# RWKV-6 attention followed by a squared-ReLU MLP on one core: another way to column sums, and a new written-out order

## The chip, the cores and the metric

The kernel runs on one core of a Trainium2 chip. A core has five engines that run side by side, each with its own in-order queue of instructions: TensorE (PE, matrix products), VectorE (DVE), ScalarE (ACT), GpSimd (POOL) and SyncE (SP), which here only issues transfers. The metric is the time on the device in microseconds (us), a median over runs. A profile is taken of one further execution. Its span runs from the first to the last instruction of the program.

## What is computed

The inputs r, k, v, w have the shape (4 batches, 8 heads, 768 steps, 48). For each batch and head a 48 x 48 state is carried over time; the result y is read as x with 3072 rows (batch and time) and 384 columns (heads x 48), and goes through an MLP:

```
for t in range(S):
    cur = einsum('bhd,bhe->bhde', u * kt, vt)
    y[t] = einsum('bhd,bhde->bhe', rt, state + cur)
    state = wt * state + einsum('bhd,bhe->bhde', kt, vt)

h = x @ w_in                      # 384 -> 2048
g = s * max(h, 0)**2 + b
out = g @ w_out                   # 2048 -> 384
```

The term b is constant, so `b @ w_out` is b times the sum of each column of w_out, one row of 384 numbers that is added to every row of the result.

## The kernel before

**Chunks and tiles.** Time is cut into 24 chunks of 128 rows; chunks 0 and 1 are packed, that is, they hold the even and odd steps of the first 256 rows of one batch. Two chunks make a tile T of 256 rows for the MLP; there are 12 tiles.

**A chunk n**, in the names of the written order. Inputs come by `load n.0` (w), `.1` (r), `.2` (k), `.3` (v), issued on SP. `ln` (ACT, L313) takes logarithms of w. `cum` (PE, L383 to L397) multiplies them with two triangular matrices, which gives running sums before and up to each row with opposite signs, and with one-column products (L391) gives the total of the chunk for each of the 384 columns, four columns of numbers. `exp` (ACT, L404 and L408) takes exponentials E of the sums and `lam` of the totals. `mul` (DVE, L424) multiplies r and k with E into `prd`. `tr` and `tev` transpose prd, on PE and ACT for chunks 0 to 8, by a transposing transfer on SP (L480) for the others. `mt` (PE, L516; L505 for packed chunks) makes the products of r and k for each head, `msk` (DVE, L527) masks them, `ymm` (PE, L570 and L579; L549 and L559 for packed chunks) multiplies them with v and adds what the state gives. `rkp`, `rku` (POOL), `cd` (DVE) and `yd` (POOL) make the term with u, and `yev` (DVE, L624) adds it to what `ymm` gave: this is x. `xtr` and `xev` transpose x (PE and ACT; for chunks from 12 a transfer, L490). `dmm` (PE, L611; L598 for packed chunks), `sup` (DVE), `l2` (POOL, L437, from lam) and `st` carry the state on. `vb` makes a bf16 copy of v.

**A tile T.** `g1 T.i` (PE, L721, eight groups of six products) multiplies x with w_in, `relu` (ACT, L734) and `sq` (ACT, L744, or DVE, L746, chosen piece by piece in the order) make g, `g2 T.i` (PE, L765, eight groups of four) multiplies with w_out, `oev` (DVE, L776) scales with s and adds the constant row, `store` (SP) writes out.

**Weights** come in four pieces each, `li0` to `li3` (w_in, L692) and `lo0` to `lo3` (w_out, L702), and are cast to bf16 by `ci` and `co`. The `colsum i` (PE, L801) of a piece follows `co i`: four products of a matrix of ones with 384 columns of w_out, which leaves the column sums in all 128 rows at once. `csevac` (ACT, L810) scales them with b into `bconst`.

**The order.** All engines' instructions stand in one text, `ORDER`, word by word; `pl.order` only checks that what a step needs stands before it. Each engine takes its own steps in this order. A suffix `@A` or `@D` puts a step on ACT or DVE. A word `+n` is n products of zeros on PE (`warm`, L1048) whose result nobody reads; all 54 of them stand before the first `g1`. Buffers are rings: PSUM ring A has one buffer (`cum`, `mt`), B two (`tr`, `ymm`, `dmm`, `xtr`, column sums), h and o two each; E has two. The costs and due times in the calls of `add` do not act on a run whose order is written out. Only the dependencies and rings in them are checked against the text.

At the start SP issues

```
load0.0 load0.2 load0.1 load2.0 load_u load3.0 load3.1 load2.1 load2.2 load3.2 load0.3
load3.3 lo0 li0 load2.3 li1 li2 load4.0 small li3 lo1 load4.1 load4.2 load5.0 lo2 load6.0 lo3
```

where load0 and load1 are one packed transfer of 384 KB for each input, other loads have 192 KB and weight pieces 768 KB.

## Time and profile before

| | us |
|---|---|
| median of 6 runs (range) | 191.26 (190.82 to 193.73) |
| the profiled execution's own time | 191.15 |
| its span | 189.4 |
| PE busy | 180.7 (95%) |
| ACT busy | 140.5 (74%) |
| DVE busy | 127.2 (67%) |
| POOL busy | 105.4 (56%) |
| SP's transfers, as a share of 16 transfer engines' span | 94.2% |
| products of `g1` (576) and `g2` (400), busy | 77.7 and 74.7 |
| products of zeros (54), busy | 9.4 |
| products of the column sums (16), busy | 3.3 |

Busy times of products overlap, since each is counted until its end and the next starts before. What a product costs PE is read from one start to the next in the timeline. A line of a timeline gives the start, the time until the last of the group has ended, the engine, the line of the kernel, the operation, the tiles (out, in), the shape and the count; in brackets how long the engine had nothing to do before it and what it waited for. The chain is followed back from the last instruction, at each step to what released it. SPq in it is the queue of SP, DMA a transfer from its issue to its landing.

### The profile page before, as it was taken

What the parts mean: (1) busy time and instruction counts of PE and PEld (TensorE: products, weight loads), DVE (VectorE), ACT (ScalarE), POOL (GpSimd) and SP (SyncE); (2) the same over time, 40 slices, a digit from 0 to 9 for tenths busy, and PEclk for the clock granted to TensorE, in tenths of its full rate; (3) what the DMA queues carried; (4) which work ended last, traced back from release to release, by engine and by line L of the source; (5) the groups of instructions that cost most, each with busy time, mean ns of one, the idle gap of its engine ahead of it and who ended that gap; (6) DMA issues with size and microseconds to landing.
All of it is one profiled execution on the core that took longest, in us unless ns stands there. A gap on an engine that the chain in (4) does not pass through costs nothing.

```text
span 189.4 us, 4916 instructions
## 1 busy us (share of the span) xinstructions
PE 180.7 (95%) x1916; PEld 141.1 (74%) x1916; DVE 127.2 (67%) x198; ACT 140.5 (74%) x268; POOL 105.4 (56%) x138
## 2 busy tenths in 40 slices
PE   6897997999999999999999999999999999999992
PEld 3575795877778887778877777778778777887872
DVE  7459793457869949978686648956677876670241
ACT  2595869897698999958988988649689778483830
POOL 3688763703949965969566795069334767100000
PEclk9999999999999999999999999999999999999998
DMA  6999998999999999999999899997997999630033
GB/s 148 222 201 336 336 332 219 254 254 197 155 201 199 213 198 173 219 172 213 138 212 215 134 211 161 192 207 137 218 197 121 217 164 188 146 109 0 0 128 125
DMA packets 122601, 35.32 MB, mean 187 GB/s; under 512 B 117329, under 2 KB 120530, under 8 KB 122578
## 3 DMA queue, kind: packets, MB, share of 16 engines
q1 hardware_dynamic: 122578, 35.01, 94.2%
q8 instruction: 15, 0.25, 0.6%
q14 instruction: 8, 0.07, 0.1%
HBM read 25.17 MB, written 4.72 MB: 158 GB/s over the span
## 4 chain that ended last, share of the span: by engine, by line
PE 71%; SPq 18%; DMA 7%; ACT 1%; issue 1%; DVE 0%
PE o_ps L765 29%; PE h_ps L721 29%; SPq L292 12%; DMA wi_st<-in_moe_w_in_dram 4%; PE mt_ps L516 3%; DMA wt<-in_w_dram 3%; PE y_ps L579 2%; SPq L300 2%; PE y_ps L570 2%; SPq L702 2%; SPq L841 2%; PE cums L383 1%; PE cums L386 1%; PE d_ps L611 1%; ACT w_in L825 1%
## 5 line engine op out<-in xcount | busy, mean ns | idle before, releaser
L721 PE MATMUL h_ps<-xT,w_in 128*128 128x256 bf16 x576 | 77.7, 273 | 1.1 <-POOL w_in L827 1.1
L734 ACT ACTIVATE rh<-h_ps 128x512 bf16<-128x512 f32 x96 | 56.9, 599 | 24.9 <-PE h_ps L721 24.2
L765 PE MATMUL o_ps<-w_out,gT 128*128 128x384 bf16 (+1 forms) x400 | 74.7, 320 | 0.0
L721 PEld LDWEIGHTS <-w_in 128*128 128x128 bf16 x576 | 60.6, 114 | 8.3 <-POOL w_in L827 1.5
L765 PEld LDWEIGHTS <-gT 128*128 128x128 bf16 x400 | 36.8, 98 | 15.8
L744 ACT ACTIVATE gT<-rh 128x512 bf16<-128x512 bf16 x65 | 39.3, 633 | 0.4
L318 POOL TENSOR_TENSOR rkp<-rkt 128x384 f32<-128x384 f32 x22 | 24.1, 1097 | 15.7 <-DMA rkt<-in_k_dram 15.1
L424 DVE TENSOR_TENSOR prd<-rkt,E 128x768 bf16<-128x768 f32 x22 | 27.2, 1236 | 7.9 <-DMA rkt<-in_k_dram 7.0
L527 DVE TENSOR_TENSOR mt_sb<-mt_ps,tri_strict 128x1024 bf16<-128x1024 f32 x22 | 26.8, 1220 | 7.8 <-PE mt_ps L516 7.7
L347 POOL TENSOR_TENSOR yd<-vt,cd 128x384 bf16<-128x384 f32 x22 | 19.9, 910 | 12.9 <-DVE cd L341 7.4
L324 POOL TENSOR_TENSOR rku<-rkp,u_bc 128x384 f32<-128x384 f32 x24 | 26.9, 1125 | 0.4
L746 DVE TENSOR_TENSOR gT<-rh 128x512 bf16<-128x512 bf16 x31 | 16.3, 537 | 9.1 <-ACT rh L734 9.1
L404 ACT ACTIVATE E<-cums 128x768 bf16<-128x768 f32 x24 | 19.5, 812 | 3.4 <-PE cums L391 1.2
L624 DVE TENSOR_TENSOR x_sb<-y_ps,yd 128x384 bf16<-128x384 f32 x24 | 13.3, 554 | 12.1 <-PE y_ps L579 8.6
L776 DVE SCALAR_TENSOR_TENSOR o_sb<-o_ps,s_bc,bconst 128x384 f32<-128x384 f32 (+1 forms) x25 | 14.8, 596 | 7.7 <-PE o_ps L765 7.7
L661 POOL TENSOR_TENSOR st<-stmp,l 128x384 bf16<-128x384 bf16 x16 | 14.9, 934 | 1.6 <-DVE stmp L652 1.6
L313 ACT ACTIVATE logw<-wt 128x384 bf16<-128x384 f32 x22 | 11.4, 524 | 4.6 <-DMA wt<-in_w_dram 4.4
L437 POOL TENSOR_TENSOR l<-lam,par 128x8 f32<-128x8 f32 x20 | 6.9, 347 | 13.6 <-ACT lam L408 13.6
L341 DVE TENSOR_REDUCE cd<-rku 128x8 f32<-128x384 f32 x24 | 13.0, 544 | 2.1 <-POOL rku L324 2.0
L652 DVE TENSOR_TENSOR stmp<-d_ps,st 128x384 bf16<-128x384 f32 x16 | 8.8, 551 | 4.2 <-PE d_ps L611 2.7
L1048 PE MATMUL warm_ps<-warm_sb 128*128 128x256 bf16 x54 | 9.4, 309 | 1.1 <-DVE warm_sb L1005 1.1
L473 ACT COPY RK<-trps 128x1024 bf16<-128x1024 bf16 x7 | 7.1, 1015 | 2.6 <-PE trps L450 2.6
(90 smaller groups left out, 175.8 us busy)
## 6 DMA issues: line engine op xcount, KB each, us to landing
out_dram<-o_sb SPq DMA_DIRECT2D x23, 192.0 KB, 3.2
wt<-in_w_dram SPq DMA_DIRECT2D x22, 192.0 KB, 4.4
rkt<-in_r_dram SPq DMA_DIRECT2D x22, 192.0 KB, 4.6
rkt<-in_k_dram SPq DMA_DIRECT2D x22, 192.0 KB, 4.6
vt<-in_v_dram SPq DMA_DIRECT2D x22, 192.0 KB, 3.8
wo_st<-in_moe_w_out_dram SPq DMA_DIRECT2D x4, 768.0 KB, 6.2
wi_st<-in_moe_w_in_dram SPq DMA_DIRECT2D x4, 768.0 KB, 8.5
pkt<-in_w_dram SPq DMA_DIRECT2D x1, 384.0 KB, 3.9
```

The costliest lines, as they stand in the source:

```text
L292: nc.sync.dma_start(out=dst, in_=src[bb, :, t0 : t0 + L, :].transpose([1, 0, 2]))
L318: nc.gpsimd.tensor_tensor(out=rkp, in0=c["r"], in1=c["k"], op=ALU.mult)
L324: nc.gpsimd.tensor_tensor(out=rku.rearrange("t h d -> t (h d)"), in0=c["rkp"].rearrange("t h d -> t (h d)"), in1=u_bc, op=ALU.mult,)
L347: nc.gpsimd.tensor_tensor(out=yd, in0=c["v"], in1=c["cd"].unsqueeze(2).to_broadcast([128, H, D]), op=ALU.mult,)
L404: nc.scalar.activation(out=E, in_=ps[:, :, 0:HD], func=AF.Exp)
L424: nc.vector.tensor_tensor(out=prd[:, :, :, 0:D].rearrange("t x h d -> t (x h) d"), in0=c["rk"].rearrange("t x h d -> t (x h) d"), in1=c["E ...
L527: nc.vector.tensor_tensor(out=m.rearrange("s g p t -> s (g p) t"), in0=c["mt_ps"].rearrange("s g p t -> s (g p) t"), in1=(masks[n % 2] if ...
L721: nc.tensor.matmul(ps[:, f, :], lhsT=w_in_sb[ft // FPP][:, kt, :].rearrange("p (m j) -> p j m", j=FPP)[:, ft % FPP, :], rhs=xT[T][:, kt, : ...
L734: nc.scalar.activation(out=rh, in_=hs[T, i], func=AF.Relu)
L744: nc.scalar.activation(out=g, in_=rh, func=AF.Square)
L746: nc.vector.tensor_tensor(out=g, in0=rh, in1=rh, op=ALU.mult)
L765: nc.tensor.matmul(os_[T, k][:, cols], lhsT=gT[T][:, ft, tt * 128 : (tt + 1) * 128], rhs=w_out_sb[ft // FPP][:, ft % FPP, cols], start=(ft ...
```

## The change

- **Column sums.** `colsum` makes 48 products of one column in place of 16 of 384: a block of 128 x 128 of w_out is the stationary operand, one column of ones the moving one, and the sums come as three columns of a [128, 3] piece. `cssplit` (DVE) splits these into two bf16 parts, `csspread` (PE) spreads both over all rows by six products with the identity, and `csevac` follows as before.
- **Exponentials.** E becomes float32 and gets four more columns for the totals' exponentials, `lam`. There is code for leaving out the second product of `cum` (`incl`, `expn`) from chunk ONE on. With ONE = 24 and 24 chunks no chunk takes it.
- **Packed chunks.** `ymm` runs through both halves of the array in turn inside the loop over heads.
- **The order** is written anew as a whole. It has 84 products of zeros, all before the first `g1`. 52 squares are on ACT (65 before); `co0` is on DVE (ACT before), `ci1` on ACT (POOL before).

The head of the diff's order, and its functions:

```diff
+ONE = 24
 ORDER = """
-load0.0 load0.2 load0.1 load2.0 load_u ln0 ln1 load3.0 +13 cum0 exp0 load3.1 +8 cum1 l20 mul0
-load2.1 load2.2 ln2 rkp0 +2 u_mm load3.2 exp1 tr0 ln3 load0.3 +1 cum2 mul1 tev0 l21 u_ev load3.3
-+4 tr1 rkp1 exp2 lo0 tev1 rku1 +4 cum3 exp3 li0 mul2 +9 mt0 rku0 cd1 load2.3 tr2 msk0 rkp3 tev2
-li1 l22 +7 mt1 mul3 vb0@A vb1@A rkp2 msk1 +1 tr3 dmm0 li2 tev3 rku3 sup0 +2 mt2 st0 cd0 co0@A ymm0
-cd3 yd0 msk2 load4.0 yd1 ymm1 ci0 yev0 small rku2 xtr0 mt3 yev1 vb2 xev0 +1 xtr1 vb3 xev1 +1 dmm1
-l23 li3 +1 dmm2 sup1 g10.0 cd2 ci1 dmm3 g10.1 sup2 relu0.0 msk3 ymm2 relu0.1 lo1 yd2 sq0.0@A g10.2
-sup3 sq0.1@A g10.3 yd3 load4.1 yev2 ymm3 load4.2 ci2@D ln4 g20.4 relu0.2 xtr2 yev3 cum4 relu0.3
-sq0.2 load5.0 g10.4 xev2 sq0.3@A xtr3 g10.5 ci3 xev3 colsum0 relu0.4 lo2 relu0.5 g20.0 sq0.4 exp4
-g10.6 co1 load6.0 sq0.5@A g11.0 relu0.6 lo3 g20.1 relu1.0 g11.1 sq0.6@A mul4 load5.1 g10.7 relu1.1
...
+load0.0 load_u load0.2 load0.1 load2.0 load0.3 ln0 +15 u_mm ln1 load3.1 +1 cum0 exp0 load3.0 +5
+cum1 l20 mul0 load2.1 exp1 rkp0 +1 tr0 load2.2 ln2 mul1 tev0 +6 cum2 load3.2 u_ev +2 tr1 exp2 rku0
+li0 tev1 l21 cd0 rkp1 load3.3 vb1@A +14 mt0 vb0@A msk0 rku1 ln3 load2.3 +5 dmm0 mul2 +5 cum3
+load4.0 exp3 sup0 +5 tr2 rkp3 st0 cd1 +1 mt1 tev2 yd0 msk1 li1 rkp2 ci0 li2 +13 ymm0 mul3 li3 mt2
+l22 yev0 yd1 tr3 msk2 +1 ymm1 lo0 tev3 vb2 rku2 yev1 +2 xtr0 +1 mt3 xev0 rku3 xtr1 cd2 ln4 +1 dmm2
+xev1 sup2 yd2 vb3@A cd3 +6 g10.0 ci1@A msk3 ymm2 l23 yd3 dmm3 g10.1 yev2 relu0.0 cum4 lo1 sup3
+xtr2 relu0.1 g10.2 sq0.0 small2 sq0.1@A ci2@D dmm1 relu0.2 g10.3 load5.0 sup1 xev2 g10.4 sq0.2
+relu0.3 ci3 ymm3 relu0.4 g10.5 yev3 load4.1 xtr3 relu0.5 g10.6 co0 xev3 g10.7 relu0.6 sq0.4
+colsum0 load4.2 sq0.3@A g11.0 exp4 lo2 co1 g20.4 relu0.7 lo3 g20.0 l24 sq0.5 ln5 load4.3 colsum1
+sq0.6 relu1.0 g20.5 sq0.7 g11.1 load6.0 g11.2 relu1.1 mul4 cum5 relu1.2 g11.3 rkp4 load5.1 exp5
+g20.1 sq1.0@A co2 g11.4 relu1.3 tr4 sq1.1 relu1.4 load5.2 st3 g11.5 sq1.3@A colsum2 co3 relu1.5
+load6.1 g20.2 tev4 g20.6 vb4 small rku4 colsum3 sq1.5@A mt4 cssplit load7.0 g20.7 msk4 l25 st1
+csspread g20.3 load6.2 csevac sq1.2 dmm4 ln6 g11.6 mul5 load6.3 cum6 relu1.6 load5.3 rkp5 g11.7
...
+relu1.7 mul6 cum7 g21.0 exp7 load7.3 rkp6 yev4 tr6 sq1.7@A mt5 load9.0 sq1.4 tev6 g21.1 l27 cd5
+vb5 msk5 xtr4 ln8 rku6 load8.1 g21.2 xev4 dmm5 g21.6 vb6@A yd5 sup5 load8.2 sq1.6@A cum8 l26 ymm5
+mul7 exp8 load9.1 dmm6 g21.3 rkp7 yev5 vb7@A g21.7 load10.1 sup6 xtr5 cd6 l28 mt6 rku7 xev5
...
         c = cb[n]
         cc, _ = coords(n)
         ps = c["cum"]
-        E = work.tile([128, 2, HD], BF16, name="E", tag="E", bufs=2)
-        nc.scalar.activation(out=E, in_=ps[:, :, 0:HD], func=AF.Exp)
-        c["E"] = E
-        if cc < NCH - 1:
-            lam = work.tile([128, HP], FP32, name="lam", tag="lam")
-            nc.scalar.activation(out=lam, in_=ps[:, 0, HD : HD + HP], func=AF.Exp)
-            c["lam"] = lam
+        E = work.tile([128, 2, HD + HP], FP32, name="E", tag="E", bufs=2)
+        c["E"], c["lam"] = E, E[:, 0, HD : HD + HP]
+        if n < ONE:
+            nc.scalar.activation(out=E[:, :, 0:HD], in_=ps[:, :, 0:HD], func=AF.Exp)
+            if cc < NCH - 1:
+                nc.scalar.activation(
+                    out=c["lam"], in_=ps[:, 0, HD : HD + HP], func=AF.Exp
+                )
+            return
+        w = HD + HP if cc < NCH - 1 else HD
+        nc.scalar.activation(out=E[:, 0, 0:w], in_=ps[:, 0, 0:w], func=AF.Exp)
+
+    def incl(n):
+        c = cb[n]
+        t = work.tile([128, HD], FP32, name="inc", tag="inc", bufs=1)
+        nc.vector.tensor_tensor(
+            out=t.rearrange("t (h d) -> t h d", h=H),
+            in0=c["cum"][:, 0, 0:HD].rearrange("t (h d) -> t h d", h=H),
+            in1=c["lw"][:, :, 0:D],
+            op=ALU.add,
+        )
+        c["inc"] = t
+
+    def expn(n):
+        c = cb[n]
+        nc.scalar.activation(
+            out=c["E"][:, 1, 0:HD], in_=c["inc"], func=AF.Exp, scale=-1.0
+        )
 
     def mult(n):
         c = cb[n]
...
         c["y_ps"] = ps
         if packed(n):
             n0 = n - n % 2
-            for half in range(2):
-                rows = slice(64 * half, 64 * half + 64)
-                if half:
-                    for p in range(HP):
-                        nc.tensor.matmul(
-                            ps[rows, p * 2 * D : (p + 1) * 2 * D],
-                            lhsT=cb[n0]["RK2"][:, n % 2, p, rows],
-                            rhs=cb[n0]["st_out"][:, p, :],
-                            start=(p == 0),
-                            stop=False,
-                        )
-                for h in range(H):
-                    p, sg = divmod(h, 2)
-                    for q in range(2):
+            cols = slice(64 * (n % 2), 64 * (n % 2) + 64)
+            for p in range(HP):
+                nc.tensor.matmul(
+                    ps[64:128, p * 2 * D : (p + 1) * 2 * D],
+                    lhsT=cb[n0]["RK2"][:, n % 2, p, 64:128],
+                    rhs=cb[n0]["st_out"][:, p, :],
+                    start=(p == 0),
+                    stop=False,
+                )
+            for h in range(H):
+                p, sg = divmod(h, 2)
+                for q in range(2):
+                    for half in range(2):
+                        rows = slice(64 * half, 64 * half + 64)
                         nc.tensor.matmul(
                             ps[rows, h * D : (h + 1) * D],
-                            lhsT=cb[n0 + q]["mt"][rows, sg, p, 64 * (n % 2) : 64 * (n % 2) + 64],
+                            lhsT=cb[n0 + q]["mt"][rows, sg, p, cols],
                             rhs=cb[n0 + q]["vb"][rows, h, :],
                             start=(half == 0 and h == 0 and q == 0),
                             stop=(h == last and q == 1),
...
             rows = out[bb * S + cc * L : bb * S + (cc + 1) * L]
         nc.sync.dma_start(out=rows[:, cols], in_=o_sb[:, cols])
 
+
+
     def colsum(i):
         if i == 0:
-            os_["cs"] = psB.tile([128, d_model], FP32, name="cs_ps", tag="B")
+            os_["cs"] = psB.tile([128, 512], FP32, name="cs_ps", tag="B")
         for ft in range(i * FPP, (i + 1) * FPP):
-            nc.tensor.matmul(
-                os_["cs"],
-                lhsT=ones,
-                rhs=w_out_sb[i][:, ft % FPP, :],
-                start=(ft == 0),
-                stop=(ft == FT - 1),
-            )
+            for kt in range(KT):
+                nc.tensor.matmul(
+                    os_["cs"][:, kt : kt + 1],
+                    lhsT=w_out_sb[i][:, ft % FPP, kt * 128 : (kt + 1) * 128],
+                    rhs=ones[:, 0:1],
+                    start=(ft == 0 and kt == 0),
+                    stop=(ft == FT - 1 and kt == KT - 1),
+                )
+
+    def cssplit():
+        ps = os_.pop("cs")[:, 0:KT]
+        for x in range(2):
+            if x == 0:
+                nc.vector.tensor_copy(out=cs_sum[:, 0], in_=ps)
+            else:
+                nc.vector.tensor_tensor(
+                    out=cs_sum[:, 1], in0=ps, in1=cs_sum[:, 0], op=ALU.subtract
+                )
+
+    def csspread():
+        ps = psB.tile([128, d_model], FP32, name="csb_ps", tag="B")
+        for kt in range(KT):
+            for x in range(2):
+                nc.tensor.matmul(
+                    ps[:, kt * 128 : (kt + 1) * 128],
+                    lhsT=cs_sum[:, x, kt : kt + 1].to_broadcast([128, 128]),
+                    rhs=identity,
+                    start=(kt == 0 and x == 0),
+                    stop=(kt == KT - 1 and x == 1),
+                )
+        os_["cs"] = ps
...
-            [("A", [("exp", n)])], P, lat=0.2, slack=SL)
-        add(("exp", n), "ACT", 0.82, expo, (n,), [("cum", n)],
-            [("E", [("mul", n)])], P - 3)
+            [("A", [("exp", n), ("inc", n)] if one else [("exp", n)])], P, lat=0.2, slack=SL)
+        add(("exp", n), "ACT", 0.47 if one else 0.82, expo, (n,), [("cum", n)],
+            [("E", [("mul", n)] + ([("l2", n)] if keep else []))], P - 3)
+            add(("exn", n), "ACT", 0.44, expn, (n,), [("inc", n), ("exp", n)], [], P - 3)
-            [("exp", n), ld(1), ld(2)]
+            [("exn" if one else "exp", n), ld(1), ld(2)]
...
-        add(("colsum", i), "PE", 0.65, colsum, (i,),
+        add(("colsum", i), "PE", 0.31, colsum, (i,),
-            [] if i else [("B", ["csevac"])], BIG + 2005 + i, lat=0.2)
-    add("csevac", "ACT", 0.45, csevac, (), [("colsum", NPIECE - 1), "small2"], [], 50.0)
+            [] if i else [("B", ["cssplit"])], BIG + 2005 + i, lat=0.2)
+    add("cssplit", "DVE", 0.25, cssplit, (), [("colsum", NPIECE - 1)], [], 49.0)
+    add("csspread", "PE", 0.33, csspread, (), ["cssplit"], [("B", ["csevac"])],
+        BIG + 2010, lat=0.2)
+    add("csevac", "ACT", 0.45, csevac, (), ["csspread", "small2"], [], 50.0)
```

## The prediction

> **What bounds the kernel now.** I read the page's busy shares and 40 slices first, then the chain that ended last, then the timeline of TensorE and the queue of SyncE (SP). The shares and slices:
>
> ```profile
> span 189.4 us, 4916 instructions
> ...
> PE 180.7 (95%) x1916; PEld 141.1 (74%) x1916; DVE 127.2 (67%) x198; ACT 140.5 (74%) x268; POOL 105.4 (56%) x138
> ...
> PEclk9999999999999999999999999999999999999998
> DMA  6999998999999999999999899997997999630033
> ```
>
> Two resources are full: PE, and the transfers until about slice 32 (152 us). The clock is full in every slice. The chain in order of time says which of them ends last:
>
> ```profile
> 13.71 7.97 DMA wi_st<-in_moe_w_in_dram
> 21.70 1.47 ACT w_in L825
> 23.17 0.77 ACT xT L687 x2
> ...
> 46.13 5.40 DMA wt<-in_w_dram
> 51.55 0.53 ACT logw L313
> 52.69 0.67 PE o_ps L765 x4
> ```
>
> Transfers lead to 52 us, PE alone after that. The first piece of w_in lands at 21.68 and the first `g1` starts at 24.32. PE's later waits, and the spacing of the products in question, are in its timeline:
>
> ```profile
> 10.63 0.24 PE L391 MATMUL cums<-ones,logw 128*128 128x1 bf16 x4
> 10.73 0.60 PE L1048 MATMUL warm_ps<-warm_sb 128*128 128x256 bf16 x4
> ...
> 13.92 0.42 PE L505 MATMUL mt_ps<-RK 48*64 48x128 bf16 x16
> ...
> 20.24 1.09 PE L559 MATMUL y_ps<-vb,mt_sb 64*64 64x48 bf16 x32
> 21.26 0.36 PE L549 MATMUL y_ps<-st,RK 128*64 128x96 bf16 x4
> ...
> 30.26 0.81 PE L801 MATMUL cs_ps<-w_out,ones 128*128 128x384 bf16 x4
> 30.91 0.81 PE L765 MATMUL o_ps<-w_out,gT 128*128 128x384 bf16 x4
> 32.83 1.50 PE L721 MATMUL h_ps<-xT,w_in 128*128 128x256 bf16 x12 [1.10 <-POOL w_in L827]
> ```
>
> From 24.32 until its last product (185.9) PE has two real gaps: 1.27 us before 32.83 (start to start, less the product's own time), for the last piece of w_in, and 0.22 us at 51.9, for load8.0. So 161.6 us hold 160.1 of work. Nothing else idles PE, so a better order can win only at the start, in those gaps, or by less PE work.
>
> The transfers are one stream. Landing times in the trace step by 1.05 us per small load (44.47, 45.45, 46.50, 47.56) and by 2.0 to 3.1 us per weight piece, and adding such steps (0.65 a store, 0.9 and 1.7 for the two transposes) follows the landings from 39 to 144 us within about 1 us. The stream never empties until about 164 us. It is nearly a second bound.
>
> **The change, part by part.**
>
> *Column sums.* Removed: 16 products of 384 columns; four take 30.26 to 30.91, so 4 x 0.65 = 2.6 us. Added: 48 one-column products, each with its own weights. The nearest row is L391, the same form: four from 10.63 to 10.73, 25 ns each, and 54 such spacings have this median. 48 x 0.0255 = 1.22 us. Against it, the Trainium skill, "TensorE: Matmul & The Clock Gate", Back-to-back issue gap, says a stream of weight load and product pairs sustains about 81 ns each at 128 columns, and that the small gap leaves the weight load out. By that rule 48 cost 3.9 us and the edit loses 1.3. I take the row: L579 keeps 25 ns over eight in a row with eight weights. The range keeps the 3.9. The spread adds six 128-column products, 56 ns by L450: 0.33. Sum -1.05 us, all on PE's path. `cssplit` is two DVE operations of three columns, near the 60 ns of `par`, plus hand-over: under 0.5 us, covered by `mt4` and `g20.7` (about 1 us) ahead of `csspread`. DVE waits in it for colsum3; `msk4` behind it needs `mt4`, later on PE anyway.
>
> *Packed products.* `ymm` of chunks 0 and 1 alternates halves. Now 32 take 1.02 us (20.24 to 21.26). L505, which alternates already, starts pairs 4 ns apart and then waits 30. 16 x 36 ns = 0.58 saves 0.44 each, 0.9 in both. The Trainium skill, "TensorEngine Tiling (Array Packing)", Gotcha 1, says row tiles can't write one PSUM bank together: then nothing is saved. L505 writes one bank from both halves, so the row wins. It lies before the first `g1`.
>
> *Exponentials.* `ONE = 24` and `n < ONE` holds for every chunk: the branches with `incl` and `expn` never run, and no product or exponential goes away. E becomes float32 and lam lies in it. The f32 x bf16 product L424 has a 946 ns shortest and 1236 mean; f32 x f32 I bound between 0 and +0.2 us, hidden by DVE's idle third; uncovered, 24 x 0.2 = 4.8. I take 0, as an ACT result of 384 f32 (L810, 582 ns) is near the bf16 one (L313, 524). New wait: exp(n) also waits for `l2`(n-2) on POOL. Queued behind it on ACT are relus, which free h. The closest is exp8 behind l26, three places ahead in the order and behind vb5 and yd5 on POOL; my sum puts both near 52 us. 0 taken, 1 us at most.
>
> *Zeros.* 84 instead of 54, all ahead of g1. At 0.11 us, 30 more are 3.3 us of PE in gaps. The clock is full now, so no gain; +6 before g10.0 costs 0.65 where it isn't covered.
>
> *Squares.* ACT has 52 instead of 65: 13 x 0.63 = 8.2 us leave ACT, 7.0 (13 x 0.54) go to DVE, which stays near 71%. co0 goes to DVE (0.96), ci1 from POOL to ACT (1.47). PE waits for none of these now: 0.
>
> *Order, the start.* On SP load_u moves to place 2 (no data to speak of; u_mm's 0.84 us now precede cum0 and cost it about 0.4). load0.3 moves ahead of the small loads (+1.5 us on load2.2, 12.9 to 14.5, still before DVE is ready for `mul2` at 15.2). li0 passes load3.3 and lo0: 21.68 - 2.2 - 2.0 = 17.5. li3 passes lo0 and small: 30.96 - 2.3 - 1.0 = 27.7. The w_out pieces now follow all of w_in. On POOL rku0 passes l21, rkp1 and rku1, so cd0 comes first and yd0 isn't late. On DVE and PE, end to end with the rows' durations (product 1.27 for a chunk, mask 1.21, copies 1.0, `yev` 0.55): mul1 ends near 11; tr1, tev1 and mt0 follow to 13.9; msk0 15.2; mul2 16.4; tr2 16.9; mt1 17.4; msk1 18.7, the same as now, since `mul3` moved behind it pays for the later mul2; ymm0 then starts at once (19.37 now, behind sup0 at 19.3, which moved ahead of msk1); mul3 20.0; yev0 20.5; msk2 21.7; yev1 22.25; xtr1 and xev1 22.9. ci0 has long been done. With dmm2 and six zeros g10.0 starts near 23.3, 1.0 us earlier. Here yev1 on DVE has taken the place of li0 and ci0 as what comes last. ci1 on ACT ends near 25, so relu0.0 and g10.2 come near 25.8, as now. ci3 then ends near 29.3, where PE reaches g10.6: the 1.27 us gap goes.
>
> *Then the stream is late next.* From g10.0 the work is 160.1 - 1.05 + 0.34 (chunk 1's `dmm`, now behind it) = 159.4: without a stall PE ends at 182.7, 3.2 us earlier. But lo3 has only one small load fewer ahead of it: 41.45 - 1.05 = 40.4, plus a cast of 0.96 and hand-over: colsum3 at 41.5. PE, with 16.5 us of work ahead of it and 0.3 of switches, is there at 40.1: 1.4 us stalled. After that load8.0 has the same bytes ahead as now (11.9 MB) and PE comes to cum8 as it lands; tr8 fits. Gain left 1.8. Later, tiles transposed by DMA land 1.2 to 2.5 us before `mt` uses them; the tightest (chunk 21) loses 0.3 of its 1.25 by the new order and 1.2 to the earlier PE: about 0.3 us stalled. Another 0.2 for small stalls in a new order. Sum: -1.3 us.
>
> The profiled run's own time is 191.15 (span 189.4 and 1.75 around it), 0.1 under the median of 191.26. 191.15 - 1.3 = 189.85; as a median, **190.0 us**. A measurement of this kernel tells about 0.5%, 1 us, from no change.
>
> **Rivals.**
>
> *Feed-bound, no change.* If the stream is the bound to its end, PE can't end before the last transposed tile plus what follows it: PE work from g111.0 is 13.1 us instead of 12.4. The head start is stalled away: 191.2. For: 164 us of unbroken stream. Against: 2 us of slack at the last tile, and a tile made earlier is sent earlier.
>
> *Everything fits.* w_out pieces land at the 2.0 us of lo0 and li1, the thinner stretch of the stream at 30 to 35 us (0.73 busy) fills, and nothing stalls: 191.26 - 3.2 = 188.1. Against: slack of only about 1 us in a dozen places.
>
> *Slower.* The 40.4 us for lo3 still holds the present steps of the w_out pieces: about 2.0 us for lo0 and lo1, 3.07 for lo2, 2.34 for lo3. Now lo0 and lo1 follow w_in without small loads between them, and lo2 and lo3 follow each other. If all four take lo2's step, lo3 lands 1.05 + 1.05 + 0.7 = 2.8 us later, at 43.2; colsum3 starts at 44.3, and the 142.6 us of work from there (182.7 - 40.1) end at 186.9 instead of 185.9: 192.3. It decides from lo3 landing after about 42. For it: lo2's own row. Against it: lo3's step, and two pieces at 4.04 us together early on.
>
> **Chances.** Likeliest 0.42 (own range 189.0 to 190.5), everything fits 0.13, feed-bound 0.22, slower 0.23 (192.2 to 194). Faster: 0.40 + 0.13 = 0.53. Within 0.5%: 0.02 and 0.18 of feed-bound, 0.20. Slower: 0.23 + 0.04, 0.27. The range 188.3 to 192.7 leaves out about half of the fast rival and half of the slow one, 0.18 in all.
>
> **What would show it.** Right: one-column products 25 ns apart; g10.0 near 23.3; no wait before g10.6; a new PE wait for w_out's casts near 40; mt's waits below 1 us. Wrong: column sums at 80 ns; lo3 after 42; PE waiting for ACT behind an exponential; the last product no earlier than 185.9.

## The result, and the profile after

The changed kernel takes 191.18 us (median of 30 executions, 189.21 to 193.06) beside 191.81 for the kernel before (65 executions, 189.97 to 194.17). The ratio is 0.9945, with a 95% interval of 0.9926 to 0.9964: 0.55% faster, about 1.1 us, where 1.3 were forecast. The two medians differ by 0.6 us only, because the ratios in this document leave out executions that lie more than 1.5% above the fastest of their own program. Times of one and the same program spread over about 2 to 5 us. Single profiles are compared below from their first `g1` on, because what lies ahead of it varies most; behind it one program can still differ by 1.2 us, as the second profile of the changed kernel will show.

The profiled execution took 189.96 us with a span of 188.1 (before: 191.15 and 189.4). Its page, shares and slices:

```profile
span 188.1 us, 5062 instructions
...
PE 181.8 (97%) x1984; PEld 143.0 (76%) x1984; DVE 129.6 (69%) x214; ACT 134.5 (71%) x254; POOL 104.5 (56%) x138
...
PEclk9999999999999999999999999999999999999999
DMA  5998999989999899999997999959699797730212
```

PE is still the full engine. The transfers are nearly full to about 155 us, with two thin slices in between (5 tenths from 122 us, 6 from 132). The squares have left ACT (140.5 to 134.5 us) without moving anything that ends last. The clock row reads full in every slice, as before; the experiments show what it doesn't say.

PE's timeline, at the places that the prediction named (start, us until the last of the group has ended, engine, line, operation, tiles, shape, count, idle time and what ended it):

```profile
18.97 0.36 PE L572 MATMUL y_ps<-st,RK 128*64 128x96 bf16 x4
19.26 0.69 PE L584 MATMUL y_ps<-vb,mt_sb 64*64 64x48 bf16 x32
19.88 0.40 PE L541 MATMUL mt_ps<-RK 48*128 48x128 bf16 x8
...
23.81 0.60 PE L746 MATMUL h_ps<-xT,w_in 128*128 128x256 bf16 x4
...
26.53 0.82 PE L746 MATMUL h_ps<-xT,w_in 128*128 128x256 bf16 x6 [0.16 <-ACT rh L759]
...
31.64 0.44 PE L829 MATMUL cs_ps<-ones,w_out 128*128 128x1 bf16 x12
31.94 0.61 PE L746 MATMUL h_ps<-xT,w_in 128*128 128x256 bf16 x4
...
41.92 0.45 PE L829 MATMUL cs_ps<-ones,w_out 128*128 128x1 bf16 x12 [0.49 <-DVE w_out L880]
...
43.30 0.50 PE L851 MATMUL csb_ps<-identity,cs_sum 128*128 128x128 bf16 x6
43.63 0.49 PE L790 MATMUL o_ps<-w_out,gT 128*128 128x384 bf16 x2
```

Read the starts. Twelve one-column products take from 31.64 to 31.94, 25 ns each; their spread takes 0.33 us (43.30 to 43.63). The `ymm` of a chunk goes from 18.97 to 19.88, 0.91 us, and that of the other chunk takes 0.90. Before, the two stood back to back and took 2.79 us (19.37 to 22.16), so 0.98 us are gone:

```profile
19.37 0.65 PE L559 MATMUL y_ps<-vb,mt_sb 64*64 64x48 bf16 x16
...
21.54 0.68 PE L559 MATMUL y_ps<-vb,mt_sb 64*64 64x48 bf16 x16
22.16 0.34 PE L672 MATMUL xt_ps<-identity,x_sb 128*128 128x128 bf16 x3
```

The first `g1` starts at 23.81 instead of 24.32. The wait of 1.27 us for w_in's last piece is gone, and a new one stands at 41.9, where `colsum3` waits for the cast of w_out's last piece: start to start 0.655 us more than the products ahead of it need. The chain in order of time names what ends last there:

```profile
17.95 6.53 DMA wi_st<-in_moe_w_in_dram
24.51 1.48 ACT w_in L876
...
33.08 7.79 DMA wo_st<-in_moe_w_out_dram
40.90 0.97 DVE w_out L880
```

The last product ends at 184.63 instead of 185.86. Of these 1.23 us, 0.51 lie ahead of the first `g1`. The stretch behind it fell from 161.54 to 160.82 us: products and their switches from 159.92 to 159.37, and waits from 1.62 to 1.45. (A wait is what the distance between two starts has beyond the usual one for that pair of products.)

### The profile page after: what moved, and what is told of

Its sections match the earlier page's. It is cut to its first block, busy times and chain, and to the rows that moved or that the text cites. A ratio compares the mean times of both kernels' runs of the same rounds, so it can differ in the third digit from the quotient of the medians.

```text
span 188.1 us, 5062 instructions
## 1 busy us (share of the span) xinstructions
PE 181.8 (97%) x1984; PEld 143.0 (76%) x1984; DVE 129.6 (69%) x214; ACT 134.5 (71%) x254; POOL 104.5 (56%) x138
## 4 chain that ended last, share of the span: by engine, by line
PE 72%; SPq 12%; DMA 10%; ACT 1%; issue 1%; DVE 1%; ACTq 0%
PE o_ps L790 31%; PE h_ps L746 28%; SPq L295 9%; DMA wo_st<-in_moe_w_out_dram 4%; DMA wi_st<-in_moe_w_in_dram 3%; PE mt_ps L541 3%; DMA wt<-in_w_dram 3%; PE y_ps L604 2%; PE y_ps L595 2%; SPq L303 2%; PE cums L386 2%; PE cums L390 2%; PE d_ps L636 1%; ACT w_in L876 1%; PE trps L475 1%
## 5 line engine op out<-in xcount | busy, mean ns | idle before, releaser
L746 PE MATMUL h_ps<-xT,w_in 128*128 128x256 bf16 x576 | 74.7, 273 | 0.2 <-ACT rh L759 0.2
L321 POOL TENSOR_TENSOR rkp<-rkt 128x384 f32<-128x384 f32 x22 | 26.8, 1218 | 15.8 <-DMA rkt<-in_k_dram 15.6
L769 ACT ACTIVATE gT<-rh 128x512 bf16<-128x512 bf16 x52 | 31.9, 627 | 0.5
L449 DVE TENSOR_TENSOR prd<-rkt,E 128x768 bf16<-128x768 f32 x22 | 25.1, 1142 | 4.8 <-ACT E L410 2.8
L771 DVE TENSOR_TENSOR gT<-rh 128x512 bf16<-128x512 bf16 x44 | 19.8, 469 | 7.9 <-ACT rh L759 7.8
L410 ACT ACTIVATE E<-cums 128x768 f32<-128x768 f32 x24 | 19.4, 808 | 7.4 <-issue 2.9
L1107 PE MATMUL warm_ps<-warm_sb 128*128 128x256 bf16 x84 | 13.6, 300 | 1.1 <-DVE warm_sb L1064 1.1
L462 POOL TENSOR_TENSOR l<-E,par 128x8 f32<-128x8 f32 x20 | 6.8, 338 | 11.3 <-ACT E L412 9.3
L878 POOL CAST vb<-vt 128x384 bf16<-128x384 f32 x11 | 6.4, 578 | 11.5 <-DMA vt<-in_v_dram 10.0
L1107 PEld LDWEIGHTS <-warm_sb 128*128 128x128 bf16 x84 | 8.1, 106 | 3.3 <-DVE warm_sb L1064 1.1
## 6 DMA issues: line engine op xcount, KB each, us to landing
out_dram<-o_sb SPq DMA_DIRECT2D x23, 192.0 KB, 2.8
wt<-in_w_dram SPq DMA_DIRECT2D x22, 192.0 KB, 4.0
rkt<-in_r_dram SPq DMA_DIRECT2D x22, 192.0 KB, 4.1
rkt<-in_k_dram SPq DMA_DIRECT2D x22, 192.0 KB, 3.9
vt<-in_v_dram SPq DMA_DIRECT2D x22, 192.0 KB, 3.9
```

The costliest lines, as they stand in the source:

```text
L321: nc.gpsimd.tensor_tensor(out=rkp, in0=c["r"], in1=c["k"], op=ALU.mult)
L410: nc.scalar.activation(out=E[:, :, 0:HD], in_=ps[:, :, 0:HD], func=AF.Exp)
L449: nc.vector.tensor_tensor(out=prd[:, :, :, 0:D], in0=c["rk"], in1=c["E"][:, :, 0:HD].rearrange("t x (h d) -> t x h d", h=H), op=ALU.mult,)
L746: nc.tensor.matmul(ps[:, f, :], lhsT=w_in_sb[ft // FPP][:, kt, :].rearrange("p (m j) -> p j m", j=FPP)[:, ft % FPP, :], rhs=xT[T][:, kt, : ...
L769: nc.scalar.activation(out=g, in_=rh, func=AF.Square)
L771: nc.vector.tensor_tensor(out=g, in0=rh, in1=rh, op=ALU.mult)
```

## The experiments

The theory to test was that of the prediction's sum: PE's own work, plus waits for a nearly full stream of transfers, set the time, and each part is worth what its instructions take. The first rival is that PE alone sets it, the second that the transfers do. A third, that TensorE's full speed begins at different moments, came up with the first four traces and is tested from the fifth run on.

### Column sums

The kernel before with the new column sums alone:

```diff
-            ... 4 products per piece: ones as weights, 384 columns of w_out
+            ... 12 products per piece: a block of w_out as weights, one column of ones
-load5.3 colsum3 msk4 load6.1 rkp5 g11.6 csevac load6.2 relu1.5 g20.6 sq1.3
+load5.3 colsum3 cssplit msk4 load6.1 rkp5 g11.6 load6.2 relu1.5 g20.6 csspread csevac sq1.3
```

> The kernel before with the new column sums alone, in its own order (cssplit behind colsum3, csspread and csevac behind g20.6). Two bounds (mine): colsum0's saving of 0.35 us is lost in the wait for the last w_in piece at 32.8, those of colsum1 and colsum2 (0.7) in a new wait of about 0.5 us for the cast of lo3 ahead of colsum3, since that cast ends only 0.2 us before PE comes now; colsum3's saving pays for the spread. Gain 0.2 us, at most 0.4: ratio 0.998 to 1.000. PE alone bounds: all of 1.05 us counts, ratio 0.9945, no new wait. The transfers alone bound: 1.000.

Measured: 191.05 us (15 executions, 187.99 to 192.89), ratio 0.9926 (0.9887 to 0.9965). That would be 1.4 us (0.7 to 2.2) less than the kernel before, but the ratio rests on six of the 15 executions, and the median of all lies above the 190.58 of the kernel before on this chip. What spreads them shows in the page of the profiled one (192.55 us):

```profile
PEclk9999858999999999999999999999999999999999
```

From 22.9 to 29.7 us TensorE ran at half clock, and the mean granted clock of this execution is 0.980. Seven of the 15 read 0.991 or less, of the kernel before nine of 54. The others compare like with like: eight with a median of 189.64 against 45 with 190.46, 0.8 us less. That fits the forecast of 1.05 better than 0.2, but it is one small sample. That a transfer takes the gain back is not seen in the profile (no wait at w_in's last piece nor at `colsum3`), in which PE comes there late.

The changed kernel with the old column sums:

```diff
-            ... 12 one-column products per piece, cssplit, csspread
+            ... 4 products of 384 columns per piece
```

> The changed kernel with the old column sums, same order without cssplit and csspread. Two bounds: colsum0 to colsum2 take 1.05 us more ahead of colsum3, whose wait of 0.65 us for the cast of lo3 goes; then 0.35 more for colsum3 and 0.33 less for the spread: 0.4 us slower than the changed kernel, last product at 185.05 instead of 184.64, ratio 0.997. PE alone: 1.05 us slower, 185.7, ratio 1.000.

Measured: 192.76 us, ratio 1.0102 (1.0067 to 1.0138), later than either theory allowed. Part of it isn't the column sums: in its profile the first `g1` comes at 25.77, 2 us later than in that of the changed kernel, and nothing ahead of `g1` differs between the two programs. From there to the end it needs 161.65 us instead of 160.82. PE's products and switches alone, without waits, take 160.6 in it and 159.4 to 159.6 in five profiles with the changed kernel's work behind `g1`. So the edit takes about 1.1 us from PE's work, as forecast, and something ahead of `g1` varies by 2 us.

### The wait for w_out's last piece

`colsum3` behind `mt4` and one group of `g1`, so that PE has work while the cast ends:

```diff
-small rku4 colsum3 sq1.5@A mt4 cssplit load7.0 ... dmm4 ln6 g11.6 mul5
+small rku4 mt4 g11.6 colsum3 sq1.5@A cssplit load7.0 ... dmm4 ln6 mul5
```

> The changed kernel with mt4 and g11.6 moved ahead of colsum3 on PE, which puts 1 us of ready work in front of its wait. Two bounds with slack behind this place: the 0.65 us wait goes and stays gone, last product at 184.0, ratio 0.991. Transfers bound further on too: the wait comes back at a later load (cum7, cum8, tr7, tr8), last product 184.4 to 184.6, ratio 0.994.

Measured: 192.33 us, ratio 1.003 (1.0 to 1.0059). Beside the changed kernel's 0.9945 that is a loss of some 1.6 us, not a gain. Its PE timeline shows where:

```profile
41.98 0.40 PE L541 MATMUL mt_ps<-RK 48*128 48x128 bf16 x8 [0.39 <-ACT RK L498]
...
42.99 0.44 PE L829 MATMUL cs_ps<-ones,w_out 128*128 128x1 bf16 x12
...
45.52 0.32 PE L386 MATMUL cums<-logw,tri_strict 128*128 128x384 bf16 x1 [0.26 <-ACT logw L316]
...
47.04 0.62 PE L475 MATMUL trps<-identity,prd 128*128 128x128 bf16 x8 [0.27 <-DVE prd L449]
```

`colsum3` no longer waits; `mt4`, `cum6`, `tr5` and `tr6` do, 1.8 us between 41 and 51 with a smaller wait at 48.7. `mt4` is not ready before 41.98 itself. And `colsum3` now ends 1 us later, and `csevac` behind it; ACT takes its steps in order, so the logarithm for `cum6` comes later too (44.96 for 44.31 in the changed kernel):

```profile
44.48 0.58 ACT L861 ACTIVATE bconst<-csb_ps,b_bc 128x384 f32<-128x384 f32 x1 [2.03 <-PE csb_ps L851]
44.96 0.51 ACT L316 ACTIVATE logw<-wt 128x384 bf16<-128x384 f32 x1
```

So the wait was traded for others. It isn't the whole difference: in this profile the first `g1` comes at 22.95, and 1.2 us are waited away at 27 and 30 for casts of w_in, which the edit doesn't touch. A head start of 0.9 us was lost there.

Half of each weight piece loaded and used twice, with the same casts and products; the other half of the weights is left out of the computation:

```diff
-            out=st, in_=moe_w_in[:, i * PW : (i + 1) * PW]
+            out=st[:, :, 0 : PW // 2], in_=moe_w_in[:, i * PW : i * PW + PW // 2]
...
-            out=st, in_=moe_w_out[i * FPP * 128 : (i + 1) * FPP * 128, :]
+            out=st[:, 0 : FPP // 2, :], in_=moe_w_out[i * FPP * 64 : (i + 1) * FPP * 64, :]
```

> The changed kernel with half of each weight piece loaded and used twice (the cast reads the half twice over, so it and all products stay as they are; the result is not the reference's). 3.1 MB, about 8 us of the stream, are gone by 40 us. Two bounds: the waits at g10.2 (0.3), xtr3 (0.2), colsum3 (0.65) and xtr near 65 us (0.26) go, the first g1 stays at 23.8 since yev1 sets it; last product near 183.4, ratio 0.988. Transfers alone bound: several us, last product before 181, ratio below 0.975. PE alone: 184.3, ratio 0.992.

Measured: 190.5 us, ratio 0.9952 (0.9921 to 0.9983). From the first `g1` to the end its profile has 160.22 us, 159.4 of them work and 0.8 waits, and `colsum3` starts without a wait. With 3 MB less to move no more is won than these waits: behind the first `g1` PE's own work sets the time. The rival in which the transfers bound the kernel to its end is out (it wanted below 0.975). The 22 times say more than their median. They fall into two groups with nothing between: ten from 188.28 to 189.07 and twelve from 190.47 to 191.16, 2.2 us apart. The profile is of the upper group, with TensorE's products at half speed until 12.2 us and the first `g1` at 25.58. No profile shows the lower group.

### Zeros and the start of full speed

In the first four traces the same products ahead of `g1` take twice as long in some executions as in others. The changed kernel once more, unchanged:

> The changed kernel as it is, once more, beside the four that follow from it. If the full speed of TensorE begins at a different moment in each execution (near 3.8 us in some, near 11.9 us in others), its times fall into two groups about 1.8 us apart, some 189.5 and 191.3, and the ratio stays near 0.9945. If that was chance in four profiles, the times form one group within 0.5 us, and the ratio is again 0.9945.

Measured: 191.14 us (189.46 to 192.5), ratio 0.9975 (0.9936 to 1.0015). The times do not form two clean groups, but they spread over 3 us. Its profile is of an execution with a late start of full speed. PE's timeline in the first profile of this kernel,

```profile
4.36 1.19 PE L899 MATMUL u_ps<-u_row,one_row 1*128 1x384 f32 x2
...
5.61 0.49 PE L371 MATMUL cums<-logw,hs_pos 128*128 128x384 bf16 x2
5.93 0.33 PE L371 MATMUL cums<-logw,hi_neg 128*128 128x384 bf16 x1
6.10 0.33 PE L371 MATMUL cums<-logw,hs_neg 128*128 128x384 bf16 x1
```

and in this one:

```profile
4.37 1.64 PE L899 MATMUL u_ps<-u_row,one_row 1*128 1x384 f32 x2
5.94 0.39 PE L1107 MATMUL warm_ps<-warm_sb 128*128 128x256 bf16 x1
6.13 0.85 PE L371 MATMUL cums<-logw,hs_pos 128*128 128x384 bf16 x2
6.77 0.53 PE L371 MATMUL cums<-logw,hi_neg 128*128 128x384 bf16 x1
7.09 0.53 PE L371 MATMUL cums<-logw,hs_neg 128*128 128x384 bf16 x1
```

Products of 384 columns start 162 ns apart in the one and 320 in the other. Here full speed begins at 9.46 us, and the first `g1` comes at 25.14 instead of 23.81. In both profiles the clock row reads 9 in all slices. From the first `g1` to the end this execution needs 162.03 us, 1.2 more than the first one of the same program. Most of it is waits (2.4 us instead of 1.45), the longest 0.93 at 57.1, while `colsum3` waits 0.22 only: single waits move from execution to execution.

All 84 zero products left out:

```diff
-load0.0 load_u load0.2 load0.1 load2.0 load0.3 ln0 +15 u_mm ln1 load3.1 +1 cum0 exp0 load3.0 +5
+load0.0 load_u load0.2 load0.1 load2.0 load0.3 ln0 u_mm ln1 load3.1 cum0 exp0 load3.0
...
```

> All 84 zero products left out, nothing else. The prediction's step (the clock is full from the start, the zeros bring nothing): the six ahead of the first g1 go, so it starts 0.2 us earlier or the same, ratio 0.9935 to 0.9945. The other theory (unbroken work on TensorE decides when its products run at full speed): half speed until at least 12 us in every execution, first g1 at 25.6 us or later instead of 23.8, ratio about 1.003 or above, and no group of times near 189.5.

Measured: 193.39 us, ratio 1.0086 (1.0054 to 1.0118), 2.2 us more than the changed kernel on the same chip. The page's clock row and PE's timeline:

```profile
PEclk9999999999999999999999999999999999999999
```

```profile
26.53 1.44 PE L745 MATMUL h_ps<-xT,w_in 128*128 128x256 bf16 x6 [0.25 <-ACT xT L711]
...
28.61 1.15 PE L745 MATMUL h_ps<-xT,w_in 128*128 128x256 bf16 x5
29.60 0.33 PE L385 MATMUL cums<-logw,tri_strict 128*128 128x384 bf16 x1
29.76 0.33 PE L389 MATMUL cums<-logw,ntri_incl 128*128 128x384 bf16 x1
```

Six products of `g1` last 1.44 us where they last 0.82 otherwise: PE runs at half speed to 29.6 us, at a clock that the page gives as full. The prediction's reason for the zeros fell here.

26 zeros at the start, and `u_mm` out of their way:

```diff
-ln0 +15 u_mm ln1 load3.1 +1 cum0 exp0 load3.0 +5 cum1 l20 mul0 load2.1 exp1 rkp0 +1 tr0 load2.2
+ln0 +26 ln1 load3.1 +1 cum0 exp0 load3.0 +5 cum1 l20 mul0 load2.1 exp1 rkp0 +1 tr0 u_mm load2.2
```

> 26 zero products instead of 15 at the start, and the float32 product u_mm (1.2 us in that gap) moved behind chunk 0's transposes, so that the first cumulative sums follow the zeros at once. If unbroken work decides when full speed begins: half speed ends by 8 us in every execution, the slower group of times goes, and the ratio is 0.988 to 0.991. If the start of full speed depends on something outside the program: the same two groups as the changed kernel, ratio 0.9945, up to 0.3 us more for a late cum0.

Measured: 190.65 us (189.8 to 191.86), ratio 0.9942 (0.9909 to 0.9974). Half speed ends at 5.0 us in its profile, and its times spread over 2.1 us instead of 3.0. The early end is that of the first expectation, the ratio that of the second. The interval reaches into that of the unchanged kernel, so a gain in time is not shown.

The same with 23, and four zeros instead of six ahead of the first `g1`:

```diff
-ln0 +15 u_mm ln1 ... xev1 sup2 yd2 vb3@A cd3 +6 g10.0
+ln0 +23 ln1 ... tr0 u_mm load2.2 ... xev1 sup2 yd2 vb3@A cd3 +4 g10.0
```

> The changed kernel with 23 zero products at the start instead of 15, u_mm behind chunk 0's transposes, and 4 zero products ahead of the first g1 instead of 6. It follows the run with 26, whose zeros held cum0 up by 0.3 us (5.88 instead of 5.61) and whose last zeros ended 0.15 us behind xev1. If the zeros' length is all that is wrong there: first g1 at 23.8 (24.17 with 26), ratio 0.991 to 0.993. If 23 leave a break before full speed in some executions: times spread over 2 us again, ratio 0.994 to 0.996. If transfers take the head start back: first g1 at 23.8, but a wait of over 0.6 us at colsum3 and the ratio of the run with 26, 0.994.

Measured: 191.74 us, ratio 0.9999 (0.9959 to 1.0038). Half speed lasts to 6.7 us in the profile and the first `g1` comes at 24.96: the spread over more than 2 us is that of the second expectation, but the ratio is above all three. It is no improvement on 26, nor on the changed kernel. Six of the twelve executions have a mean granted clock of 0.990 or 0.991 and lie at 192.06 to 193.8, the six others at 189.58 to 191.43: in half of them TensorE seems to have fallen back to half clock, as in the first experiment's profile. With 26 zeros none of twelve did.

The kernel before with 23 zeros at its start instead of 13:

```diff
-ln0 ln1 load3.0 +13 cum0 exp0 load3.1 +8 cum1
+ln0 ln1 load3.0 +23 cum0 exp0 load3.1 +8 cum1
```

> The kernel before with 23 zero products at the start instead of 13, nothing else. If full speed begins late in some of its executions and their path passes through TensorE's work before the first g1: its slower times go, ratio 0.993 to 0.997. If the landing of the first piece of w_in (21.7 us) and its cast hold the first g1 anyway: first g1 at 24.3, ratio 0.998 to 1.001. This tells how much of the gain by more zeros belongs to the changed kernel's order.

Measured: 191.79 us, ratio 0.9995 (0.9957 to 1.0033). Its first `g1` starts at 24.24. The second expectation held: in the old order the first piece of w_in holds the first `g1`, and a quicker PE ahead of it wins nothing. The trace shows a second thing. PE's timeline of the kernel before, at the wait of 1.27 us that the prediction counted on (its line is shown there), reads in this run of the same order:

```profile
30.33 0.81 PE L801 MATMUL cs_ps<-w_out,ones 128*128 128x384 bf16 x4
30.98 0.81 PE L765 MATMUL o_ps<-w_out,gT 128*128 128x384 bf16 x4
31.63 1.47 PE L721 MATMUL h_ps<-xT,w_in 128*128 128x256 bf16 x12
```

There is no wait. w_in's last piece landed at 29.35 instead of 30.96, with nothing changed in the transfers. Instead `tr6` finds PE idle for 0.67 us at 49.5.

### Packed products, exponentials, and the order

The changed kernel with `ymm` in its old loops, half by half:

```diff
-                for q in range(2):
-                    for half in range(2):
+            for half in range(2):
+                ... for h in range(H): for q in range(2):
```

> The 32 products of ymm in their old order (all of one half of the array, then all of the other), which is 0.4 us more for each pair of chunks' product, and the same for every later chunk pair that goes this way. The prediction's step (both ymm before the first g1 and on its path): first g1 up to 0.9 us later, 24.2 to 24.7 in an execution with the early full speed, and the end 0.5 to 0.9 us later: ratio 0.997 to 0.999. The rival (VectorE's chain sets the first g1, the products are covered): first g1 within 0.2 us of 23.8, ratio 0.9945 to 0.9955.

Measured: 192.52 us, ratio 1.0056 (1.0024 to 1.0088), 1.4 us more than the unchanged kernel on the same chip. In its profile the first `g1` comes at 26.39, 1.25 us later than in the one above with the same start of full speed (9.5 us). PE's timeline:

```profile
20.33 0.68 PE L584 MATMUL y_ps<-vb,mt_sb 64*64 64x48 bf16 x16
20.95 0.36 PE L574 MATMUL y_ps<-st,RK 128*64 128x96 bf16 x4
21.23 0.68 PE L584 MATMUL y_ps<-vb,mt_sb 64*64 64x48 bf16 x16
21.85 0.40 PE L541 MATMUL mt_ps<-RK 48*128 48x128 bf16 x8
```

Sixteen products of one half take 0.62 us up to the next group, as long as 32 in alternation. Both chunks lose 0.62, and all of it arrives at the first `g1`. The rival in which VectorE's chain covers the products is out. (From there to the end this profile has 162.43 us, close to the other's 162.03.)

The changed kernel with E in bfloat16 and `lam` apart:

```diff
-        E = work.tile([128, 2, HD + HP], FP32, name="E", tag="E", bufs=2)
+        E = work.tile([128, 2, HD], BF16, name="E", tag="E", bufs=2)
+        ... lam = work.tile([128, HP], FP32), as before
```

> The changed kernel with its exponentials in bfloat16 and the decay totals apart, as before. The prediction's step (0): same time as the changed kernel, ratio 0.9945 to 0.9975. The other reading (the products of chunks 0 and 1 took 754 ns each before and 556 now, four of them one behind the other on the way to the first g1): first g1 0.4 to 0.8 us later than the changed kernel's in an execution with the same start of full speed, ratio 0.998 to 1.001.

Measured: 190.49 us, ratio 0.9954 (0.9918 to 0.999); first `g1` at 23.49 and 160.90 us from there. No cost and no gain of float32 is seen. The other reading rested on a chance: of the four products of the first two chunks, the second takes 1.35 us in four profiles (both first ones, this run and the kernel before with 23 zeros) and 0.55 in the ten others, with either type of E. The means of 754 and 556 ns come from that; what lengthens it stays open.

The kernel before, in its own order, with both edits of PE's products:

```diff
 (column sums as in the first experiment, and)
-            for half in range(2): ... for h in range(H): for q in range(2):
+            for h in range(H): for q in range(2): for half in range(2):
```

> The kernel before with both edits of TensorE's products (one-column sums with their spread, and ymm in alternating halves), in its own order. If w_in's first piece holds the first g1 there, ymm brings nothing and the column sums at most 1.05 us: first g1 at 24.3, ratio 0.9925 to 0.996. If TensorE holds it: ymm brings 1.2 us more, first g1 at 23.1 to 23.5, ratio 0.987 to 0.990. If transfers bound the kernel to its end: 0.999 or above.

Measured: 189.43 us (188.42 to 190.14, six runs), ratio 0.9867 (0.9811 to 0.9923). This is faster than the kernel before. The changed kernel's interval just doesn't meet this one (0.9926 and 0.9923), but it was measured at another time. On the same chip the six executions stand 1.1 us below the changed kernel with E in bfloat16 (twelve from 189.3 to 192.66), with intervals that overlap by 0.0005. So that this kernel is also faster than the changed one is likely, from six executions. From PE's timeline:

```profile
4.85 0.89 PE L369 MATMUL cums<-logw,hs_pos 128*128 128x384 bf16 x2 [0.84 <-DVE hi_neg L1059]
...
20.55 0.69 PE L560 MATMUL y_ps<-vb,mt_sb 64*64 64x48 bf16 x32
...
24.60 0.60 PE L722 MATMUL h_ps<-xT,w_in 128*128 128x256 bf16 x4
...
31.49 1.47 PE L722 MATMUL h_ps<-xT,w_in 128*128 128x256 bf16 x12
33.26 0.81 PE L766 MATMUL o_ps<-w_out,gT 128*128 128x384 bf16 x4 [0.29 <-DVE w_out L854]
...
41.06 0.45 PE L803 MATMUL cs_ps<-ones,w_out 128*128 128x1 bf16 x12
```

Full speed begins at 10.0 us here, as late as in the profile of 25.14 above, and yet the first `g1` comes at 24.60. `cum0` starts at 4.85, because `u_mm` doesn't stand ahead of it, and not at 6.13. `colsum3` starts at 41.06 without a wait, and from the first `g1` to the end there are 160.10 us, the least of all. In the first experiment's profile, the same order with the old `ymm`, full speed began at 9.8 and the first `g1` came at 25.89 (there PE also fell back to half speed at 22.9, which can be up to 1.5 us of the way to 25.89, so this pair doesn't tell what `ymm` earns). So neither expectation was right as a whole: the time is that of the second, but the first `g1` is not at 23.1 to 23.5. It may be that w_in's first piece holds the first `g1` where full speed is early, and PE where it is late, and that `ymm` earns in the second case; no pair of profiles here shows it.

## Why the prediction was right

The total was right, at 1.3 us against about 1.1, and part of that is luck. The prediction's sum was 23.3 to the first `g1`, 159.4 of work and 1.9 of waits, 184.6; the profile has 23.81, 159.37 and 1.45, 184.63. The work was right by its reasons. The start was half a microsecond late and the waits half a microsecond short, and the two misses cancel. And this profile has an early full speed, of which the sum knew nothing; the second one ends at 187.18. Step by step:

| step | forecast, us | what the runs showed |
|---|---|---|
| column sums | -1.05 | 48 x 25 ns and 0.33 for 2.6; 1.1 of PE's work when undone |
| `ymm` | -0.9 ahead of `g1` | 0.98 from PE's timelines; 1.25 at the first `g1` when undone |
| E in float32, squares | 0 | no cost found for E; no PE wait for a square |
| 30 more zeros | 0 to +0.65 | leaving all 84 out costs 2.2; the 30 alone not tested |
| first `g1` | 23.3 | 23.81, and 25.14 with full speed late |
| wait for w_in | -1.27 | gone, but gone too in runs of the old order |
| PE's work from `g1` | 159.4 | 159.37 |
| wait at `colsum3` | +1.4 | 0.655 |
| `g10.2` | 25.8 | 26.53, a wait of 0.32 |
| transposed tiles, small stalls | +0.5 | 0.48 in two waits (29.8, 65.2), none at `mt21` |

*Column sums.* Here the row stood against the page, and the row decided: 25 ns in 37 of 44 spacings (the longest 39), over runs of twelve with twelve weights. The 81 ns of the Trainium skill ("TensorE: Matmul & The Clock Gate", Back-to-back issue gap) would have made the edit cost 1.3 us. The page gives them for 128 moving columns, and these products move one, so the figure didn't fit the case; but the six products of the spread, which do move 128 with weights of their own, start 56 ns apart. `cssplit` took 165 and 164 ns and was covered as forecast.

*Packed products.* L584 kept alternating at 0.62 us per 32, close to the 0.58 taken from L505, though both halves write one PSUM bank. The two chunks save 0.98, for 0.9 forecast. The undone run loses more, 1.24, though its products are 32 ns apart as before: in the new order the two `ymm` stand apart, and each pays 0.62 for each half, switches included. In the old order one chunk's second half ran into the other's first, without a switch and with some starts 5 ns apart.

*Zeros: the step whose reason failed.* "The clock is full now, so no gain" was read off the clock row. That row doesn't show at which speed the products run ahead of the first `g1`. The spacing of the zeros did: in the kernel before the first ones start 213 ns apart and later ones 109, in the very timeline from which the prediction took its rows (the line at 10.73, shown there, is of the later ones):

```profile
1.05 2.95 PE L1048 MATMUL warm_ps<-warm_sb 128*128 128x256 bf16 x13 [1.05 <-DVE warm_sb L1005]
```

And the page that the prediction cites says it (the Trainium skill, "TensorE: Matmul & The Clock Gate", Part 1): the array starts at half rate, full rate comes after one busy window of about 3.4 us, and the window runs freely, so the moment varies. By the clock row, leaving the zeros out brings 0 to 0.65 us; by the page, PE's work ahead of `g1` takes up to twice as long wherever zeros don't keep it busy. The run says +2.2. What the change's 30 further zeros bring over the 54 before, no run here tells apart; the last section has a hint that they keep TensorE from falling back.

*The start.* Up to `yev1` the forecast held within 0.3 us (mask 1 at 18.80 for 18.7, mask 2 at 21.75 for 21.7, `yev1` at 22.51 for 22.25). The last leg was mis-sized. It was taken for 0.65 us to the end of `xev1`; the copy waits on ACT behind a logarithm and ends at 23.64, as ACT's timeline of the changed kernel shows:

```profile
22.74 0.53 ACT L316 ACTIVATE logw<-wt 128x384 bf16<-128x384 f32 x1
23.17 0.47 ACT L712 COPY xT<-xt_ps 128x384 bf16<-128x384 bf16 x1
```

The six zeros cost 0.17 of their 0.65. The 0.4 us for `u_mm` ahead of `cum0` were right when full speed is early (5.61 for 5.25). When it is late, `u_mm` takes 1.57 us and `cum0` starts at 6.13 instead of 4.85: 1.3.

*The wait at `colsum3`.* In this profile the place was right and the size half: lo3 landed at 40.87 for 40.4, but PE came at 41.27 for 40.1, since the first `g1` was 0.5 us late and 0.54 were waited away at 26.2 and 29.8. The first of those waits has the place that the prediction named (`ci1`, now on ACT, ahead of `relu0.0`), but li1 landed at 24.48, so the cast ended at 25.99 instead of near 25.

*The order.* The prediction gave it the head start and the wait of 1.27 us. That wait was a feature of one execution: w_in's last piece lands anywhere from 27.0 to 31.0 us in four profiles of the old order, and only the latest makes PE wait there. Against it stands the new wait at `colsum3` (0.655 and 0.22 in two profiles), which the profiles of the old order don't have. By the ratio of the run with both product edits, the products are worth 2.5 us in the old order (1.5 to 3.6); against only those executions of the kernel before that kept full clock (18 of 29, median 191.09) it is 1.7. What else the change does gives back about 1 us. Which part of the new order does so is argued from the traces alone: `u_mm` ahead of `cum0`, the wait for w_out's last piece, and chunk 1's `dmm` behind the first `g1` (27.28 to 27.72, 0.44 for 0.34 forecast).

*The rivals.* Feed-bound to the end: out, by the half weights. Everything fits, 188.1: the changed kernel's shortest time was 189.21. Slower by w_out's pieces: its switch was lo3 landing after 42, and it landed at 40.87.

## What to carry to other kernels

A wait in one profile is one draw: before counting its removal as a gain, ask whether the transfer that it waits for lands at the same moment in other executions. Count an edit of the engine that is full by the spacing of its instructions, with the switches around them, which held here to about 0.1 us for the column sums and `ymm`, and distrust the gain of everything that only moves. And read the speed of TensorE at the start from the distance between equal products: the clock row leaves out the half speed ahead of the first full speed.

## What was not expected of the hardware

TensorE's products ran at half speed (213 ns for 256 columns, 320 for 384, instead of 109 and 162) from the first product at 1.05 us to a moment between about 4 and 12.2 us that differed between executions of nearly the same program: ahead of 5.7 in the first profiles of both kernels and in two variants of the changed one; 9.5, 9.8, 10.0 and 9.5, and 12.2 twice, in others with 13 or 15 zeros at the start; 5.0, 4.8 and 6.7 in the three with 23 or 26. Without zeros it was 29.6. The clock row of the page shows nothing of this.

In the first experiment's profile half speed came back from 22.9 to 29.7, though PE had worked without a gap since 18.3, and that the row does show. The mean granted clock counts it too: 6.8 us at half clock are 1.8% of 190.8, and it reads 0.980. By this figure the kernel before falls back often. Of its 115 executions beside the experiments, 85 read 0.995 or more (median 190.8 us), 16 about 0.99 (192.0) and 14 about 0.98 (193.3), which is 1.2 us for each hundredth. Of the 42 executions of the changed kernel, one reads below 0.995. So part of the spread of the kernel before seems to be fall-back, and that of the changed kernel is not. Which part of the change keeps it away, the further zeros or the order, was not tested.

The Trainium skill's free-running window of 3.4 us ("TensorE: Matmul & The Clock Gate", Part 1) would explain early, 9.5 and 12.2 as one, two or three windows, if `u_mm` with its single row doesn't count as busy, and the 6.8 us of the fall-back as two; no run here tests that.

Sixteen 64-row products in one half of the array take as long (0.62 us) as 32 that alternate between the halves, though both halves write one PSUM bank.
